# Inner products of mixer 1 on four PSUM banks, and a warm-up of TensorE in parts gated by the first tile's statistics

## Chip, cores, metric

One core of a Trainium2 chip. The metric is the device time of one launch in microseconds (us). A time quoted for a kernel is the median of its runs; a span is the length of the one profiled run, some 2 us shorter than its time. All runs used here are fast (a granted clock of 0.99 to 1.00).

## The reference, cut

```python
h  = x + linear_attention(layernorm(x), wqkv, wo)     # x: 2048 x 1024, 32 heads
h2 = h + mixer(layernorm(h), w1, b1, w2, b2)
# mixer: its own layernorm, then over the tokens:
#   u = gelu(einsum("bsd,sf->bdf", h, w1) + b1)       # "mixer 1": 2048 -> 3584
#   y = einsum("bdf,fs->bds", u, w2) + b2             # "mixer 2": 3584 -> 2048
```

## The kernel before

The matrix products run as seven block products instead of eight (Strassen-like), in two levels. A *unit* of mixer 1 makes two pairs of output tiles. Three of its outer products (1, 5 and 2) are again split in seven: these are the *inner products*, written by the class `Inner`. An inner product has the running results a, b, c and e, each 128 x 256 fp32, half a bank of PSUM (the memory that the matmuls here write to). Before the change a and e lie in one bank, b and c in another:

```python
class Inner:
    def i1(self):
        ae = psz.tile([P, BANK], F32, tag="z0", bufs=1, name="psI0")
        bc = psz.tile([P, BANK], F32, tag="z1", bufs=1, name="psI1")
        self.a, self.e, self.b, self.c = ae[:, 0:HW], ae[:, HW:CW], bc[:, 0:HW], bc[:, HW:CW]
        self.mm(1, self.a, True)                       # TensorE, 4 matmuls into a
        nc.scalar.copy(self.b, self.a)
    def i6(self): self.mm(6, self.b, False); nc.scalar.copy(self.c, self.b)
    def i2(self): self.mm(2, self.a, False); self.sink(0, 0, self.a)
    def i5(self): self.mm(5, self.e, True);  ...; nc.scalar.copy(self.es[:], self.e)
    def i7(self): self.mm(7, self.c, False); self.sink_sum(1, 1, self.c, self.es[:])  # VectorE reads c
    def i3(self): self.mm(3, self.b, False); self.sink_sum(0, 1, self.b, self.es[:])  # VectorE reads b
    def i4(self): self.mm(4, self.c, False); self.sink(1, 0, self.c)
```

`Inner2`, the third inner product of a unit, adds e to two results on VectorE instead of copying it. Matmuls of an outer product are interleaved as *fill*, so that TensorE has work while other engines read PSUM:

```python
def interleave(self, n, fs, at={}):
    steps = [(f, k) for f in fs for k in range(self.sts[0].nk)]      # 16 fill matmuls in mixer 1
    t = len(steps)
    cuts = [0, (5 * t + 8) // 16, (9 * t + 8) // 16, (12 * t + 8) // 16, t]   # groups of 5, 4, 3, 4
    ...
    for f in (n.i1, "in", 0, n.i6, n.i2, 1, n.i5, n.i7, flush, 2, "mid", n.i3, "third", 3, n.i4, "out", flush):
        ...                                                           # a number is a fill group
```

At the start, TensorE runs ten matmuls on zeros (`warm_up(10)`) while the first tile of x is loaded and normalized:

```python
def warm_up(n, w=BANK):
    tiles = [acc_tile() for _ in range(5)]
    for t in range(n):
        ps = tiles[t % 5]
        pin(nc.tensor.matmul(ps[:, 0:w], lhsT=warm[:, 0:P], rhs=warm[:, 0:w], start=True, stop=True))
...
warm_up(10)
...
ln_stats(0)          # VectorE: statistics of the two halves of tile 0, then mean and variance
```

## Time and profile before

| | before |
|---|---|
| time, median (range) | 574.38 us (574.22 to 576.22, 4 runs) |
| span of the profiled run | 572.5 us |
| TensorE busy | 561.0 us, 98% |
| one unit of mixer 1 (units 2 to 5) | 24.20 us |
| mixer 1, first inner product to mixer 2's first psE matmul | 406.93 - 241.21 = 165.72 us |

The head of the profile page of the kernel before; after each engine come its busy time, its share of the span and its instructions:

```profile
span 572.5 us, 8362 instructions
...
PE 561.0 (98%) x3136; PEld 296.6 (52%) x3136; DVE 412.2 (72%) x798; ACT 278.5 (49%) x585; POOL 1.8 (0%) x8
```

TensorE (PE) is the limit: time is to be had only from its gaps, or by taking work from it. Its waits, kernel before (what waited, for what, us in total, how often, longest):

```profile
engine line waited for: us in total, times, longest us
PE psI L209 <- DVE a L209: 4.8, 11, 0.8
PE acc_t L95 <- DVE warm L87: 1.2, 1, 1.2
PE acc_t L725 <- ACT xnT L978: 0.9, 2, 0.4
PE psI L209 <- DVE e L209: 0.5, 1, 0.5
PE tp L968 <- DVE xn L704: 0.4, 1, 0.4
PE psB L801 <- DVE xs L787: 0.3, 1, 0.3
```

The rows with psI are inner products of mixer 1 (DVE is VectorE). One of these waits in the timeline of the kernel before, in order of time (start, us, engine, line, operation, how many):

```profile
307.76 0.60 PE L209 MATMUL psI<-hi,is 128*128 128x256 f16 x4
308.05 0.67 ACT L407 ACTIVATE gO<-psC,b_sb 128x512 f16<-128x512 f32 x1
...
308.19 0.81 PE L209 MATMUL psC<-hT,wq 128*128 128x512 f16 x3
308.62 0.36 ACT L255 COPY es<-psI 128x256 f32<-128x256 f32 x1
...
309.01 0.43 DVE L209 TENSOR_TENSOR a<-psI,es 128x256 f32<-128x256 f32 x1 [1.72 <-ACT es L255]
309.35 0.68 DVE L209 TENSOR_TENSOR sa<-sa,wq 128x1024 f16<-128x1024 f16 x1
...
309.49 0.60 PE L209 MATMUL psI<-hE,is 128*128 128x256 f16 x4 [0.48 <-DVE a L209]
```

Product 7 writes c at 307.76. ScalarE (ACT) is in a gelu and copies e to `es` only at 308.62, then VectorE reads c at 309.01. Product 3, which writes only b, starts at 309.49, after this read has ended. Three fill matmuls, 216 ns apart, stood between; they started at 308.19, so product 3 could have started at 308.84.

### The profile page before, as it was taken

The numbers are of one execution on the slowest core, as the hardware profiler recorded it, in microseconds if no ns is written. First come the engines' busy times: TensorE is split into PE (matmuls) and PEld (weight loads), VectorE is DVE, ScalarE is ACT, GpSimd is POOL, SyncE is SP. The second block draws the span as 40 slices with busy tenths as digits, with TensorE's granted clock in tenths as the row PEclk, the third lists the DMA queues.
The fourth block names the chain that finished last, engine by engine and source line by source line (L and its number), as shares of the span: only waits on it lengthen the run. The fifth ranks groups of instructions, "written<-read, shape, count | busy, mean of one in ns | idle before, by whom it ended". The sixth has DMA issues, their size and how long they took to land.

```text
span 572.5 us, 8362 instructions
## 1 busy us (share of the span) xinstructions
PE 561.0 (98%) x3136; PEld 296.6 (52%) x3136; DVE 412.2 (72%) x798; ACT 278.5 (49%) x585; POOL 1.8 (0%) x8
## 2 busy tenths in 40 slices
PE   8999999999999999999999999999999999999997
PEld 3444444454444444456565565655445655655643
DVE  6898887544786798877767666684979749658725
ACT  5657777667767777535446454364220410311211
POOL 1000000000000000000000000000000000000000
PEclk9999999999999999999999999999999999999999
DMA  9933432135674931104041240413792932912111
GB/s 298 292 71 81 88 72 38 19 106 173 182 230 108 302 134 73 56 1 148 1 148 59 89 147 2 148 32 97 191 260 82 250 99 77 270 61 75 37 47 46
DMA packets 86088, 67.13 MB, mean 117 GB/s; under 512 B 15762, under 2 KB 80032, under 8 KB 86048
## 3 DMA queue, kind: packets, MB, share of 16 engines
q1 hardware_dynamic: 85312, 65.94, 40.2%
q10 hardware_dynamic: 672, 0.66, 0.3%
q8 instruction: 24, 0.39, 0.3%
q14 instruction: 16, 0.13, 0.1%
q0 software_dynamic: 64, 0.01, 0.0%
HBM read 54.54 MB, written 8.91 MB: 111 GB/s over the span
## 4 chain that ended last, share of the span: by engine, by line
PE 89%; DVE 5%; ACT 2%; DMA 1%; issue 1%; SPq 0%; DVEq 0%; ACTq 0%
PE acc_t L209 18%; PE psI L209 15%; PE psB L209 14%; PE psC L209 13%; PE psB L801 4%; PE psC L801 4%; PE psA L801 4%; PE psA L209 3%; PE psB L313 2%; PE psA L313 2%; PE acc_t L1070 2%; PE psE L801 2%; PE psC L313 2%; PE acc_t L725 2%; DVE a L209 1%; DMA x_sb<-in_A_x_dram 1%
## 5 line engine op out<-in xcount | busy, mean ns | idle before, releaser
L209 PEld LDWEIGHTS <-sa 128*128 128x128 f16 x651 | 63.7, 98 | 48.4
L209 PEld LDWEIGHTS <-wq 128*128 128x128 bf16 (+1 forms) x629 | 61.0, 98 | 46.8
L209 PEld LDWEIGHTS <-is 128*128 128x128 f16 x472 | 46.0, 98 | 29.5 <-issue 10.1
L209 PE MATMUL acc_t<-wo_sb,pqT 128*128 128x512 f16 x256 | 55.6, 379 | 0.0
L209 PE MATMUL psC<-gs,wq 128*128 128x512 f16 (+2 forms) x210 | 44.9, 365 | 0.0
L209 PE MATMUL acc_t<-xnT,wq_sb 128*128 128x512 bf16 x192 | 43.4, 379 | 0.0
L209 PEld LDWEIGHTS <-pqT 128*128 128x128 bf16 x256 | 25.0, 98 | 30.5 <-issue 0.6
L171 DVE TENSOR_SCALAR e_sb<-e_sb 128x512 bf16<-128x512 bf16 x64 | 18.6, 290 | 27.9 <-ACT e_sb L167 27.3
L167 ACT ACTIVATE e_sb<-acc_t 128x512 bf16<-128x512 f32 x40 | 23.9, 597 | 24.5 <-PE acc_t L209 12.0
L801 PEld LDWEIGHTS <-xs 128*128 128x128 f16 x208 | 20.0, 98 | 23.4 <-DVE xs L787 1.3
L209 DVE TENSOR_TENSOR ot<-ot,hr 128x512 bf16<-128x512 bf16 (+2 forms) x27 | 11.2, 414 | 28.1 <-ACT ot L454 27.7
L209 PEld LDWEIGHTS <-wq_sb 128*128 128x128 bf16 x192 | 18.5, 98 | 23.0 <-issue 1.3
L350 ACT COPY psC<-psB 128x512 f32<-128x512 f32 x22 | 12.5, 570 | 35.9 <-PE psB L209 31.1
L209 DVE TENSOR_TENSOR a<-psI,a 128x256 f32<-128x256 f32 x36 | 14.7, 423 | 20.2 <-PE psI L209 18.9
L209 PE MATMUL psB<-hT,sa 128*128 128x512 f16 x112 | 28.7, 379 | 0.0
L209 PE MATMUL psC<-hT,sa 128*128 128x512 f16 x112 | 28.3, 379 | 0.0
L209 DVE BATCH_NORM_STATS2 hst<-acc_t 128x6 f32<-128x512 f32 x32 | 21.4, 692 | 9.1 <-ACT h_bf L209 8.9
L242 ACT COPY psI<-psI 128x256 f32<-128x256 f32 x25 | 8.8, 354 | 37.9 <-PE psI L209 37.5
L801 PE MATMUL psA<-wkv,xnT 128*128 128x512 bf16 x104 | 26.7, 379 | 0.0
L209 PE MATMUL psB<-hO,sa 128*128 128x512 f16 x112 | 25.3, 379 | 0.0
L246 ACT COPY psI<-psI 128x256 f32<-128x256 f32 x25 | 8.9, 357 | 33.0 <-PE psI L209 33.0
L801 PEld LDWEIGHTS <-xnT 128*128 128x128 bf16 x156 | 15.3, 98 | 18.5 <-issue 0.2
(196 smaller groups left out, 1046.4 us busy)
## 6 DMA issues: line engine op xcount, KB each, us to landing
wq<-in_B_w_dram SPq DMA_DIRECT2D x14, 1024.0 KB, 8.0
wq<-in_B_w_dram SPq DMA_DIRECT2D x8, 1792.0 KB, 9.1
xr<-in_A_x_dram SPq DMA_DIRECT2D x16, 256.0 KB, 5.1
rdb<-rd_dram SPq DMA_DIRECT2D x32, 128.0 KB, 4.0
h_dram<-h_bf SPq DMA_DIRECT2D x16, 256.0 KB, 2.0
hr<-h_dram SPq DMA_DIRECT2D x32, 128.0 KB, 2.6
out_dram<-ot SPq DMA_DIRECT2D x31, 128.0 KB, 1.7
x_sb<-in_A_x_dram SPq DMA_DIRECT2D x15, 256.0 KB, 3.1
```

What stands on the lines that cost most here:

```text
L167: pin(nc.scalar.activation(e_sb[:], src, ACT.Exp))
L171: pin(nc.vector.tensor_scalar(e_sb[:], e_sb[:], 1.0, PHI_EPS, ALU.min, ALU.add))
L209: return (lambda *a, **kw: pin(op(*a, **kw))) if self.always or Held.on else op
L242: nc.scalar.copy(self.b, self.a)
L246: nc.scalar.copy(self.c, self.b)
L313: pe.matmul(ps[:, cols], lhsT=lhs[:, k, :], rhs=mv(k)[:, cols], start=(start and k == 0), stop=(k == self.nk - 1), skip_group_check=True,)
L350: nc.scalar.copy(self.C[:], self.B[:])
L725: mm = nc.tensor.matmul(pp[:, 0:CW], lhsT=xnT[:, kt, i * P:(i + 1) * P], rhs=wkv[:, kt, c * CW:(c + 1) * CW], start=(kt == 0), stop=(kt == ...
L801: pin(nc.tensor.matmul(ps[:], lhsT=lhs[:, k, :], rhs=rhs[:, k, :], start=(start and k == 0), stop=(k == hk2 - 1), skip_group_check=True,))
L1070: nc.tensor.matmul(qp[:, 0:SW], lhsT=wq_sb[:, kt, j * P:(j + 1) * P], rhs=xnT[:, kt, u * SW:(u + 1) * SW], start=(kt == 0), stop=(kt == ND ...
```

## The change

Its intent: with c and e in banks of their own, b and c no longer meet in one bank. The tag `w` belongs to a pool of two banks that mixer 1 used only in its first unit. Mixer 2 goes back to two banks. The first unit's sums are split so that VectorE reaches the sums of e sooner. The warm-up gets longer and is cut in parts, each behind a tiny matmul that reads x, its statistics, or its mean and variance, so that TensorE works shortly before the first tile is ready however late x comes.

```diff
     class Inner:
+        banks = 4
@@
         def i1(self):
             ae = psz.tile([P, BANK], F32, tag="z0", bufs=1, name="psI0")
             bc = psz.tile([P, BANK], F32, tag="z1", bufs=1, name="psI1")
-            self.a, self.e, self.b, self.c = ae[:, 0:HW], ae[:, HW:CW], bc[:, 0:HW], bc[:, HW:CW]
+            e, c = ae, bc
+            if self.banks == 4:
+                e, c = (psw.tile([P, BANK], F32, tag="w", name=f"psI{i}") for i in (2, 3))
+            self.a, self.e, self.b, self.c = ae[:, 0:HW], e[:, HW:CW], bc[:, 0:HW], c[:, HW:CW]
@@ run_first
-            before_inner()
+            before_inner(slice(0, 2))
             self.in5.mov = self.mov5
             self.interleave(self.in5, [st.p6 for st in sts])
+            before_inner(slice(2, 4))
@@ start  (warm_up(n, behind) puts one small matmul of `behind` ahead of its n)
-            warm_up(10)
+            warm_up(6)
@@
-            ln_stats(0)
+            warm_up(2, xs[0][:, 0:CW // 8])
+            ln[0] = ln_chunks(0, xs.pop(0))
+            pin(ln[0][1](0))
+            warm_up(2, ln[0][5][:, 0, :])
+            pin(ln[0][1](1))
+            pin(ln[0][2]())
+            warm_up(2, ln[0][6][:])
@@ after mixer 1
+    Inner.banks = 2
```

More of the change, by code (lines that the diff above doesn't have):

```diff
@@ L89, with warm_up, mm @@
     make_identity(nc, ident[:])
-    def warm_up(n, w=BANK):
-        tiles = [acc_tile() for _ in range(5)]
+    warm_tiles = [acc_tile() for _ in range(5)]
+    def warm_up(n, behind=None):
+        def mm(lhsT, rhs):
+            ps = warm_tiles[0]
+            warm_tiles.append(warm_tiles.pop(0))
+            pin(nc.tensor.matmul(ps[0:lhsT.shape[-1], 0:rhs.shape[-1]], lhsT=lhsT, rhs=rhs, start=True, stop=True))
+        if behind is not None:
+            mm(behind, behind)
         for t in range(n):
-            ps = tiles[t % 5]
-            pin(nc.tensor.matmul(ps[:, 0:w], lhsT=warm[:, 0:P], rhs=warm[:, 0:w], start=True, stop=True))
+            mm(warm[:, 0:P], warm[:, 0:BANK])
     maskbd = const.tile([P, P], F32)
@@ L193, in inner_moving, with sums @@
         t2, t3, t4 = (pool.tile([P, nk // 2, HW], FP16, name=f"{name}{t}")[:] for t in (2, 3, 4))
-        def sums():
-            for o, a, b in ((t3, b22, b12), (b12, b12, b11), (t2, b22, b12), (t4, b21, t2)):
+        def sums(part=slice(0, 4)):
+            for o, a, b in ((t3, b22, b12), (b12, b12, b11), (t2, b22, b12), (t4, b21, t2))[part]:
                 dve.tensor_tensor(o, a, b, ALU.subtract)
@@ L704, in norm @@
                     return nc.vector.tensor_scalar(xn[:, cs], x_sb[:, cs], mv[:, 0:1], rstd[:, 0:1], ALU.subtract, ALU.mult)
-                return xn, stats, aggr, scale, norm
+                return xn, stats, aggr, scale, norm, st, mv
             ln = {}
@@ L716, in ln_finish @@
             def ln_finish(i):
-                xn, _, _, scale, norm = ln.pop(i)
+                xn, _, _, scale, norm, _, _ = ln.pop(i)
                 for op in scale():
```

## The prediction

> **What bounds the kernel now.** The page gives TensorE 561.0 of 572.5 us busy (98%), and the chain of waits that ended last is 89% TensorE. Only TensorE's own gaps, 11.5 us, can be won back; its waits name them. At the start 2.5 us for the first memset, normalized and transposed tiles. In mixer 1: `psI` matmuls wait 11 times on the VectorE sum `a` (4.8 us) and once on `e` (0.5 us).
>
> **The mechanism in mixer 1.** a and e share one PSUM bank, b and c the other. After product 7 (into c) VectorE adds c; product 3 (into b) waits for that read though it writes other columns. The Trainium skill ("PSUM — Partial Sum Buffer", Terms) says TensorE and another engine must not be on the same bank and quadrant at once, so the guard is per bank; the trace agrees: product 3 at 285.28 and 309.49 us starts just after the sum ends. In the third inner product (Inner2) it waits for VectorE's three queued sums (1.31 us).
>
> By start times (512-column matmuls 216 ns apart, 256-column 109 ns) the three fill matmuls before product 3 start at 308.19, so it could start at 308.84; it starts at 309.49: 0.65 us lost. The second inner product loses 0.10 us so, Inner2 0.49 us (321.96 + 0.65 against 323.09). A unit (24.2 us) has 84 x 0.109 + 64 x 0.216 = 23.0 us of matmuls: the loss agrees.
>
> **What the change does.** c and e move to two banks of the pool that mixer 1 used only in its first unit. In the new instruction order product 3 has no wait; product 4 still waits on c's sum, but 1.3 us later. No mixer instruction is added. Splitting the first unit's sums moves two 0.69 us VectorE additions behind the `e` sums.
>
> **Not all of it stays.** After the first stall is gone, the next inner product's product 6 meets ScalarE: copy psB, gelu, copy a, copy b (0.38 + 0.67 + 0.37 + 0.35 us), after a VectorE sum that follows a 0.68 us `sa` addition and so hardly moves. I estimate product 6 could go at 312.09 and the copy lands at about 312.16: 0.1 us given back per unit, 0.5 in unit 1 where VectorE is fuller.
>
> Sum (estimate): unit 0 0.6; unit 1 1.1; units 2 to 5 4 x 1.1; unit 6 0.7 (its Inner2 stall was already filled): 6.9 us.
>
> **Warm-up.** 10 matmuls at 427 ns (1.20 to 5.65 us) become 12 plus three tiny ones gated by x's first half (3.46), its statistics (4.1) and the mean/variance (5.0). The gates open before TensorE gets there, so it ends at 6.1 to 6.5 instead of 5.65, against the transposes' 6.06: 0 to +0.4 us here. The skill ("TensorE: Matmul & The Clock Gate", Part 1) says a free-running window of about 3.4 us lifts the half clock; the trace's warm-up at 427 ns and later matmuls at 216 ns agree. It is insurance for a late x, perhaps against runs like 576.22. Median: +0.1.
>
> **Prediction:** 574.25 - 6.9 + 0.1 = 567.4 us, range 565.6 to 569.6; faster by over 2%: 0.01, within 2%: 0.97, slower: 0.02.
>
> **Right if** the waits of TensorE lose the `a`/`e` rows, a unit takes 23.1 us, PE busy stays 561. **Wrong if** ScalarE's chain holds product 6 for as long as the old stall, the pool's tiles are released late, or the clock wakes later.

## The result

| | before | after |
|---|---|---|
| time, median (range) | 574.38 us (574.22 to 576.22) | 566.93 us (566.61 to 567.74) |
| ratio of fast runs | | 0.9865, 95% interval 0.9843 to 0.9888 |
| span of the profiled run | 572.5 | 566.0 |
| TensorE busy | 561.0 | 558.1 |
| one unit of mixer 1 | 24.20 | 22.98 |
| mixer 1, as above | 165.72 | 400.40 - 242.28 = 158.12 |

A ratio here is the mean time of one kernel's fast runs over that of the other's fast runs of the same rounds, so it is not quite the ratio of the medians.

The same head and waits, kernel after (its helper lines have moved from L209 to L216):

```profile
span 566.0 us, 8365 instructions
...
PE 558.1 (99%) x3127; PEld 296.6 (52%) x3143; DVE 411.3 (73%) x798; ACT 277.4 (49%) x585; POOL 1.8 (0%) x8
```

```profile
engine line waited for: us in total, times, longest us
PE acc_t L738 <- ACT rstd L714: 1.7, 1, 1.7
PE acc_t L97 <- DVE warm L87: 1.2, 1, 1.2
PE acc_t L738 <- ACT xnT L991: 0.5, 1, 0.5
PE psB L814 <- DVE xs L800: 0.3, 1, 0.3
```

All waits of psI are gone; what this view still shows lies in the first 36 us. The stall shown before, now in the timeline of the kernel after:

```profile
305.69 0.60 PE L216 MATMUL psI<-hi,is 128*128 128x256 f16 x4
...
306.12 0.81 PE L216 MATMUL psC<-hT,wq 128*128 128x512 f16 x3
306.55 0.36 ACT L267 COPY es<-psI 128x256 f32<-128x256 f32 x1
...
306.77 0.60 PE L216 MATMUL psI<-hE,is 128*128 128x256 f16 x4
306.94 0.43 DVE L216 TENSOR_TENSOR a<-psI,es 128x256 f32<-128x256 f32 x1 [1.72 <-ACT es L267]
...
307.21 1.03 PE L216 MATMUL psC<-hT,wq 128*128 128x512 f16 x4
...
308.07 0.60 PE L216 MATMUL psI<-hi,wq 128*128 128x256 f16 x4
```

Product 3 starts at 306.77, 0.65 us after the first fill matmul, before VectorE has begun to read c. Product 4, which writes c again, starts at 308.07, when the read (306.94 to 307.37) is over.

The units by stretches. Columns: stretch, its length, then for each engine its busy time and instructions, granted clock, DMA share, GB/s. First the kernel before, then after:

```profile
300.62:324.82 24.20, 23.40 (x150) 14.48 (x148) 16.41 (x36) 11.91 (x27) 0.00 (x0) 1.00 0.27 87
324.82:349.02 24.20, 23.40 (x150) 14.45 (x148) 16.40 (x36) 11.91 (x27) 0.00 (x0) 1.00 0.28 88
```

```profile
298.54:321.52 22.98, 22.98 (x150) 14.48 (x148) 16.23 (x36) 11.74 (x28) 0.00 (x0) 1.00 0.30 93
321.52:344.51 22.99, 22.99 (x151) 14.49 (x148) 16.22 (x36) 11.75 (x28) 0.00 (x0) 1.00 0.29 92
```

The same 150 matmuls took 24.20 us and take 22.98, with TensorE busy all the time. Its busy time fell by 0.42 us a unit though its work did not change: before, each stall began with a modelled tail of the last matmul that counts as busy. That is why the waits named only 5.3 us in mixer 1, while 7.60 came back.

The profiled run after is the slowest of its four, 567.74 us against 566.61 to 566.94. Its first projection matmul starts at 8.32 us, against 7.19 before. The wait is put down to `rstd` of ScalarE at 8.00 us, which is tile 1's and on which that matmul does not depend. It needs the copies `xnT` of tile 0, which end at 7.44 us, and the first half of the weights wkv, issued at 1.18 us, which took 7.0 us to land in this run and 5.1 in the run before. So some 1.1 us of this profiled run is a late transfer, and it is not part of the mixer's gain.

### The profile page after: what moved, and what is told of

Same layout as the page of the kernel before. It is cut to its first block, busy times and chain, and to the rows that moved or that the text cites. A ratio compares the mean times of both kernels' runs of the same rounds, so it can differ in the third digit from the quotient of the medians.

```text
span 566.0 us, 8365 instructions
## 1 busy us (share of the span) xinstructions
PE 558.1 (99%) x3127; PEld 296.6 (52%) x3143; DVE 411.3 (73%) x798; ACT 277.4 (49%) x585; POOL 1.8 (0%) x8
## 4 chain that ended last, share of the span: by engine, by line
PE 96%; DVE 2%; ACT 1%; issue 1%; DMA 0%
PE acc_t L216 18%; PE psI L216 16%; PE psC L216 15%; PE psB L216 15%; PE psA L216 4%; PE psC L814 4%; PE psB L814 4%; PE psA L814 4%; PE acc_t L738 3%; PE psA L325 2%; PE psB L325 2%; PE acc_t L1089 2%; PE psE L814 2%; PE psC L325 2%; PE kvps L767 1%; PE psE L325 1%
## 5 line engine op out<-in xcount | busy, mean ns | idle before, releaser
L216 PEld LDWEIGHTS <-sa 128*128 128x128 f16 x651 | 63.7, 98 | 48.5 <-issue 0.2
L216 PEld LDWEIGHTS <-wq 128*128 128x128 bf16 (+1 forms) x629 | 61.1, 98 | 46.8
L216 PEld LDWEIGHTS <-is 128*128 128x128 f16 x472 | 46.1, 98 | 21.6 <-DVE hi L216 0.4
L216 PE MATMUL acc_t<-wo_sb,pqT 128*128 128x512 f16 x256 | 55.6, 379 | 0.0
L216 PE MATMUL psC<-gs,wq 128*128 128x512 f16 (+2 forms) x210 | 45.0, 365 | 0.0
L216 PE MATMUL acc_t<-xnT,wq_sb 128*128 128x512 bf16 x188 | 43.1, 379 | 0.2
L216 PEld LDWEIGHTS <-pqT 128*128 128x128 bf16 x256 | 25.0, 98 | 30.5 <-issue 0.6
L216 DVE TENSOR_TENSOR ot<-ot,hr 128x512 bf16<-128x512 bf16 (+2 forms) x27 | 11.2, 414 | 28.1 <-ACT ot L466 27.7
L216 PEld LDWEIGHTS <-wq_sb 128*128 128x128 bf16 x192 | 18.5, 98 | 23.0 <-issue 1.3
L216 PE MATMUL psB<-hT,sa 128*128 128x512 f16 x112 | 28.7, 379 | 0.0
L216 PE MATMUL psC<-hT,sa 128*128 128x512 f16 x112 | 28.3, 379 | 0.0
L216 DVE BATCH_NORM_STATS2 hst<-acc_t 128x6 f32<-128x512 f32 x32 | 21.4, 692 | 9.1 <-ACT h_bf L216 8.9
L216 DVE TENSOR_TENSOR a<-psI,a 128x256 f32<-128x256 f32 x36 | 14.7, 422 | 17.9 <-PE psI L216 17.2
L216 PE MATMUL psB<-hO,sa 128*128 128x512 f16 x112 | 25.3, 379 | 0.0
```

The lines of the kernel that those rows point to most:

```text
L216: return (lambda *a, **kw: pin(op(*a, **kw))) if self.always or Held.on else op
```

## Experiments

Each kernel was timed in five rounds beside the kernel before (4 to 6 runs of each) and gave a correct result. e1, e3 to e6, e8 and e10 are the changed kernel with the old warm-up put back and, but for e1, one thing more edited; e2, e9, e11 and e12 keep the gated warm-up; e7 is built on the kernel before. "Mixer 1" is the stretch of the tables above, from the profiled run.

| run | time, median (range) | ratio to before | mixer 1 |
|---|---|---|---|
| e1 banks and split only | 566.65 (566.47 to 566.86) | 0.9868 | 158.12 |
| e2 gated warm-up only | 574.75 (574.26 to 574.95) | 1.0007 | 165.73 |
| e3 only c moved | 566.76 (566.64 to 566.80) | 0.9869 | 158.13 |
| e4 only e moved | 573.85 (573.49 to 573.93) | 0.9991 | 165.20 |
| e5 banks without the split | 566.70 (566.61 to 567.61) | 0.9862 | 158.13 |
| e6 Inner2 back on two banks | 569.33 (569.04 to 570.79) | 0.9910 | 160.57 |
| e7 two banks, fill cut anew | 569.18 (568.97 to 571.71) | 0.9909 | 160.61 |
| e8 x late, old warm-up | 571.38 (570.86 to 571.75) | 0.9945 | |
| e9 x late, gated warm-up | 570.26 (570.08 to 571.37) | 0.9932 | |
| e10 x later, old warm-up | 575.23 (575.18 to 575.27) | 1.0013 | |
| e11 x later, gated warm-up | 574.08 (573.30 to 574.57) | 0.9993 | |
| e12 gated warm-up, two matmuls shorter | 566.70 (566.65 to 566.96) | 0.9869 | |

### Which part carries the gain: e1 and e2

```diff
 # e1, on the changed kernel
-            warm_up(6)
+            warm_up(10)
-            (the gated parts)
+            ln_stats(0)
```

> The banks and the split of the first unit's sums, with the warm-up of before. Theory (the banks carry it all): 566.8 to 567.1 us, ratio to before 0.9865 within 0.001; mixer 1 from the first inner product to the last product 3 takes 148.2 us as in the changed kernel (before: 156.2). Rival (the gated warm-up carries part): above 567.9 us.

Measured 566.65 us, ratio 0.9868. That is 0.15 us below the expected range, which was set around the 566.93 of the change; the ratio is as expected. The expectation's 148.2 us is another stretch than the table's: it fits the end of the last product 4 (389.10 + 0.44 - 241.34 = 148.20 us in e1, and 156.2 in the kernel before). It is 8.0 us shorter and the table's only 7.60, because before, two of mixer 2's matmuls (0.43 us) already ran ahead of the last product 3 and so filled part of that wait.

```diff
 # e2, on the changed kernel
-        banks = 4
+        banks = 2
-            before_inner(slice(0, 2))
+            before_inner()
-            before_inner(slice(2, 4))
```

> The gated warm-up alone, two banks, sums unsplit. Theory: 574.2 to 574.6 us, ratio 1.000 within 0.001, and all of the eleven waits of TensorE on the sum a (4.8 us by the profile) stay. Rival: 573.5 us or less, or the slow single runs near 576 vanish while before still shows them in the same rounds.

Measured 574.75 us, ratio 1.0007 (0.9993 to 1.0020), a little over the range that was expected; all eleven waits on `a` (4.8 us) are there. So the banks with the split carry the gain, and the warm-up carries none of it. It may cost something: the trace of e2 shows TensorE still warming up when the first tile is ready. Start of e2 on TensorE:

```profile
1.19 2.74 PE L97 MATMUL acc_t<-warm 128*128 128x512 bf16 x6 [1.19 <-DVE warm L87]
3.87 0.26 PE L97 MATMUL acc_t<-x_sb 128*64 128x64 bf16 x1
4.06 1.03 PE L97 MATMUL acc_t<-warm 128*128 128x512 bf16 x2
5.02 0.20 PE L97 MATMUL acc_t<-st 128*6 128x6 f32 x2
5.16 0.99 PE L97 MATMUL acc_t<-warm 128*128 128x512 bf16 x2
6.08 0.19 PE L97 MATMUL acc_t<-mv 128*2 128x2 f32 x2
6.20 0.60 PE L97 MATMUL acc_t<-warm 128*128 128x512 bf16 x2
6.64 0.61 PE L980 MATMUL tp<-ident,xn 128*128 128x128 bf16 x8
```

The transposes of tile 0 start at 6.64 us with no wait. In e1 they start at 6.11, and there TensorE had waited 0.46 us for the tile. The difference in time, 0.5 us between e2 and before (574.24 in these rounds) and 0.3 between the change (566.93, from other rounds) and e1, points the same way, but the intervals of the ratios do not separate them. Nor does the trace of the change show this cost: there the same warm-up matmuls ran at full speed already from 4.06 us, and the transposes started at 5.94 us.

### Which bank: e3 and e4

```diff
 # e3
-                e, c = (psw.tile([P, BANK], F32, tag="w", name=f"psI{i}") for i in (2, 3))
+                c = psw.tile([P, BANK], F32, tag="w", name="psI3")
 # e4
+                e = psw.tile([P, BANK], F32, tag="w", name="psI2")
```

> Three banks: only c moves to a bank of its own, e stays beside a; warm-up of before. Theory (product 3 waited only because b shares its bank with c, which VectorE reads): the whole gain, 566.8 to 567.3 us, no wait of TensorE on the VectorE sums in mixer 1. Rival (e beside a costs too, both have to move): 569 to 572 us with a wait of product 5 or of product 1 in its place.

> Three banks: only e moves, c stays beside b; warm-up of before. Theory: nothing is gained, 574.0 to 574.8 us, and product 3 waits for the sum of c at the same places, 0.3 to 0.8 us each. Rival (any further bank helps): 570 us or less.

e3: 566.76 us (0.04 below the range), the whole gain, and no psI row among TensorE's waits. e4: 573.85 us, and the waits are those of before, less one:

```profile
PE psI L216 <- DVE a L216: 4.8, 11, 0.8
```

So what cost was c beside b: a read of c by VectorE against a matmul that writes b in the same bank. A bank more that does not part them leaves the waits standing; e beside a costs nothing. The 0.4 us of e4 was not expected. It is the twelfth wait, that on `e` in the first unit: product 3 comes 4.98 us after the unit's first inner matmul, where it came 5.51 after it before. e4 still carries the split of the sums, and its trace shows what that does: in the kernel before, VectorE reads c at 246.25 us, behind two additions of 0.69 us that started at 244.91; in e4 these two come after the sums of e, and it reads c at 245.63. So the split has a worth while b and c share a bank; e5 asks whether it has one with four banks.

### The split of the sums: e5

```diff
-            before_inner(slice(0, 2))
+            before_inner()
             ...
-            before_inner(slice(2, 4))
```

> Four banks, warm-up of before, the first unit's four moving sums in one piece again. Theory (with c in its own bank no matmul waits for VectorE's e sums, so their place in VectorE's queue does not matter): as the banks with the split, 566.5 to 567.0 us. That the split has a worth of its own was seen with e moved alone, where unit 0's wait was gone and 0.4 us with it. Rival (the split is needed with four banks too): 567.2 us or more, a wait of 0.3 us or more in unit 0.

Measured 566.70 us and 158.13 us for mixer 1, as e1. With c in its own bank no matmul waits for those sums, and the split does nothing.

### Do the stalls add: e6

```diff
     class Inner2(Inner):
+        banks = 2
```

> Four banks for the first two inner products of a unit, two banks for Inner2, warm-up of before. Theory, from the start times of before: five stalls of 0.49 us come back (units 1 to 5; unit 6 fills its own with mixer-2 matmuls), 2.4 us: 568.9 to 569.3 us. Rival (the stalls run together, and giving one back costs nothing because another engine sets the pace of a unit): under 568 us; or (a unit's stalls add to more than their parts): over 570 us.

Measured 569.33 us, 0.03 above the range; mixer 1 takes 160.57, that is 2.45 us more than e1, against 2.4 expected. The profile's five waits sum to only 1.6 us:

```profile
PE psI L216 <- DVE a L216: 1.6, 5, 0.3
```

The loss per stall, counted from start times (0.49 us), adds up; the idle time of the waits view (0.3 us each) understates it.

### Covering the wait instead of removing it: e7

```diff
 # on the kernel before
             cuts = [0, (5 * t + 8) // 16, (9 * t + 8) // 16, (12 * t + 8) // 16, t]
+            if fs[0].__self__.nk == NSP:
+                cuts = [0, 5, 8, 13, t]
```

> The kernel before, two banks, with only the four groups of fill matmuls of mixer 1 cut anew: 5, 3, 5, 3 of the sixteen instead of 5, 4, 3, 4, so two more (0.43 us) stand between product 7 and product 3. Theory (the stall is time between product 7 and VectorE's read, to be covered by any work): 0.43 us less in each long stall, small new waits of product 5 (0.05 us), so 4 to 5 us gained: 569.3 to 570.4 us. Rival (the pace of a unit is set by ScalarE or VectorE, and the banks help by something else): within 1 us of 574.2.

Measured 569.18 us, a shade better than the range. Without any bank, only by putting two more fill matmuls between product 7 and product 3, mixer 1 falls to 160.61 us: 5.1 of the 7.6 us. This is a second and independent sign that the stall was nothing but the time from product 7 to the end of VectorE's read of c, with too little other work for TensorE in it. What stays is the rest of the stalls in unit 1 (a wait of 0.6 us) and in unit 0 (0.3) and small gaps of 0.03 to 0.07 us elsewhere: product 5, for instance, starts at 305.45 us where it could at 304.77 + 3 x 0.216 = 305.42, since one fill matmul less stands before it.

### What the gated warm-up is for: e8 to e11

In the profiled runs of before and after, x came in time (statistics from 3.46 and 3.34 us). To see the warm-up at work, x's first tile was put late:

```diff
+            pin(nc.scalar.dma_start(wkv[:, 0:hk, 0:CW], ...))      # 1 MB of weights ahead of x
+            pin(nc.sync.dma_start(wkv[:, hk:ND, 0:CW], ...))
             xs = {0: load_x(0, True)}
             xs[1] = load_x(1)
-            (the same two loads, here before the change of order)
 # e8: old warm-up, e9: gated warm-up; e10 and e11: the next 1 MB of wkv goes ahead of x as well
```

> Four banks, warm-up of before, x's first tile issued behind 1 MB of wkv, so that it lands some 2.5 us later (estimate from 0.5 MB in 5.1 us and x's 2.7 us before). The warm-up ends at 5.65 us and TensorE then has nothing until about 8.5. Theory (the gated warm-up is insurance for a late x): TensorE's clock falls back in this gap in some runs, matmuls of the first tile at 427 ns apart instead of 216, and the time spreads by 1 us or more over the runs. Rival (a gap of 3 us does not put the clock back): first matmuls at 216 ns, all runs within 0.5 us.

> The same late x with the gated warm-up. Theory: TensorE idles from 3.8 us to x's arrival, then works up to the transposes; first matmuls of the first tile 216 ns apart, time under that of the ungated kernel by 0.3 us or more, and with less spread. Rival: no difference, or slower by 0.3 us as with x in time.

> As e8, but x issued behind 2 MB of wkv, some 5 us late; TensorE idle from 5.65 us to about 11. Theory: the clock is back at half speed in every run, the first eight matmuls of tile 0 take 3.4 us instead of 1.9.

> As e9, but x issued behind 2 MB of wkv. Theory: the gated matmuls run for about 2.4 us before the transposes and may or may not raise the clock in time; if they do, the first eight matmuls take 1.9 us and the kernel beats the ungated one by 1 to 2 us; if not, they are equal within 0.5 us.

Start of TensorE in e8, then e9:

```profile
1.19 4.45 PE L97 MATMUL acc_t<-warm 128*128 128x512 bf16 x10 [1.19 <-DVE warm L87]
9.04 0.92 PE L981 MATMUL tp<-ident,xn 128*128 128x128 bf16 x8 [3.40 <-DVE xn L717]
10.11 3.22 PE L738 MATMUL acc_t<-wkv,xnT 128*128 128x512 bf16 x8 [0.15 <-ACT xnT L991]
13.16 0.61 PE L981 MATMUL tp<-ident,xn 128*128 128x128 bf16 x8
```

```profile
8.81 1.03 PE L97 MATMUL acc_t<-warm 128*128 128x512 bf16 x2
9.64 1.06 PE L981 MATMUL tp<-ident,xn 128*128 128x128 bf16 x8
10.95 2.33 PE L738 MATMUL acc_t<-wkv,xnT 128*128 128x512 bf16 x8 [0.25 <-ACT xnT L991]
13.12 0.61 PE L981 MATMUL tp<-ident,xn 128*128 128x128 bf16 x8
```

In e8 the warm-up ended at 5.65 us; the eight matmuls of tile 0 then take 3.22 us where they took 1.90 before. The granted clock of e8 in short stretches (the same columns as in the unit table) shows why:

```profile
9.20:9.40 0.20, 0.20 (x5) 0.10 (x4) 0.20 (x2) 0.00 (x0) 0.00 (x0) 1.00 1.08 343
9.40:9.60 0.20, 0.20 (x4) 0.20 (x4) 0.20 (x1) 0.13 (x1) 0.00 (x0) 0.50 1.06 338
```

The clock fell to half at 9.4 us, 3.75 us after the modelled end of the last warm-up matmul and 0.36 us after TensorE had begun again. The Trainium skill ("TensorE: Matmul & The Clock Gate", Part 1) says the array falls back to half clock after at least one idle window of about 3.4 us; e8, where TensorE was idle for 3.40 us, agrees. In e10 less was enough: by the record its clock fell at 8.15 us, 2.9 us after the modelled end of the last warm-up matmul (5.26 us). With the gated warm-up (e9) the eight matmuls take 2.33 us: by their spacing, the clock rose during them. My expectation of 216 ns for all of them was missed, and so were both spreads: e8 spans 0.9 us instead of 1 or more, and e9 spans 1.3, not less. The medians, 571.38 against 570.26 us, differ by 1.1 us in favour of gating, but the ranges overlap, and so do the intervals of the ratios (0.9933 to 0.9958 and 0.9919 to 0.9944). The traces do not show this gain: in e9 the eight matmuls start 0.84 us later, and the transposes after them start at 13.12 us against 13.16. These two profiled runs (the fastest of e8, the second slowest of e9) have spans of 569.1 and 569.0.

With x later still the case is clear: e10 575.18 to 575.27 us, e11 573.30 to 574.57. The first tile's eight matmuls and the third tile's transposes, in e10 and then in e11:

```profile
13.91 3.60 PE L738 MATMUL acc_t<-wkv,xnT 128*128 128x512 bf16 x8 [0.25 <-ACT xnT L991]
22.07 0.61 PE L981 MATMUL tp<-ident,xn 128*128 128x128 bf16 x8
```

```profile
14.21 2.34 PE L738 MATMUL acc_t<-wkv,xnT 128*128 128x512 bf16 x8 [0.25 <-ACT xnT L991]
20.91 0.61 PE L981 MATMUL tp<-ident,xn 128*128 128x128 bf16 x8
```

The eight matmuls take 3.60 us in e10 and 2.34 in e11, though the gated kernel starts them 0.3 us later; by the third tile it is 1.16 us ahead. As expected of every run, all five of e10 show the slower clock: a mean of 0.991, against 0.999 to 1.000 in e11. So the gated warm-up is insurance: it is worth about 1.1 us (575.23 - 574.08) if x is as late as here, and may cost some tenths when x is in time. How often x comes late by itself was not measured.

### A shorter gated warm-up: e12

```diff
 # on the changed kernel
-            warm_up(2, xs[0][:, 0:CW // 8])
+            warm_up(1, xs[0][:, 0:CW // 8])
-            warm_up(2, ln[0][5][:, 0, :])
+            warm_up(1, ln[0][5][:, 0, :])
```

> The changed kernel with two warm-up matmuls less, one behind x and one behind its statistics: 6 + 1 + 1 + 2 instead of 6 + 2 + 2 + 2, so ten in all as before the change, still gated. Theory (with x in time the gated warm-up costs only by running past the point where the first tile is ready, 6.64 us against 6.1 in the warm-up run): the transposes start at 6.2 us or earlier even when the clock wakes late, and the time is that of the banks alone, 566.5 to 566.8 us. Rival (the small gated matmuls or the broken rhythm cost): transposes after 6.4 us, 566.9 us or more.

Measured 566.70 us; the transposes start at 6.10 us after a wait of 0.29. That is the time of e1, the gating kept, but it is not a proof that it beats the change: 566.65 to 566.96 against 566.61 to 567.74, from different rounds. In this run the clock also rose early (the matmul at 4.68 us is at full speed), so its worst case was not seen. Its worth with a late x was not tried.

## Why the prediction was right

- **What bounds the kernel.** Right: TensorE was busy all along, and the time won is its gaps. One number of this step was off: "PE busy stays 561". It fell to 558.1 (558.7 in e1), because a gap's first 0.16 us or so had counted as busy. And "Only TensorE's own gaps, 11.5 us" was the profile's idle time, which understates the gaps; it did no harm, as the sum was made from start times.
- **The mechanism.** Right, and shown twice over: c alone in a bank of its own gives the whole gain (e3), e alone leaves eleven of the twelve waits (e4), and covering the wait by other work gives two thirds of the gain without any bank (e7). The Trainium skill ("PSUM — Partial Sum Buffer", Terms) has the rule that TensorE and another engine must not be on one bank and quadrant at once; the trace shows the wait that the program's guard for it makes. Whether the chip would have failed without the guard was not tried. Nor do the runs tell a guard by bank from one by tile: wherever b and c shared a bank, they were halves of one tile too.
- **The size of each stall.** Right: 0.65, 0.10 and 0.49 us a unit make 1.24, and a unit became 1.22 us shorter. The 0.49 of Inner2 was tested alone: five of them, 2.45 us (e6).
- **"Not all of it stays."** The mis-sized term. I took off 0.5 us in unit 1 and 0.1 us in each later unit (1.0 us in all) for ScalarE's chain of copies. In the units that the unit table shows nothing is given back: in the unit from 298.54 ScalarE's copy of b ends at 309.92, and product 6 starts at 310.02, just when its fill ends (five matmuls from 308.94). So that copy lands 0.10 us before it is needed, where I had put it 0.07 us after: my estimate was about 0.2 us too late. In unit 1, TensorE waits 0.17 us for a copy of psB. Unit by unit the gain was 0.63 us (unit 0), 1.29 (unit 1), 1.22 in each of units 2 to 5, and 0.80 (unit 6): 7.60 us instead of 6.9.
- **The warm-up.** "0 to +0.4 us" is not contradicted: the medians of e2 and e1 put its cost at 0.3 to 0.5 us without resolving it, and the trace of the change shows none. "Insurance for a late x" is right for the very late x of e10 and e11; for e8 and e9 it is not settled. That it prevents runs like 576.22 is not shown: such runs came up again in later rounds of the kernel before (576.12, 576.72), and the profile was never taken in one. What makes them slow stays open.
- **The sum.** 574.24 - 7.60 = 566.64 us for the banks (e1 measured 566.65); the change itself stands 0.3 above that, at 566.93, in other rounds; whether that is the warm-up is not resolved. The prediction of 567.4 is 0.5 too high: it took 0.7 us too little for mixer 1, mostly by giving back too much in units 1 to 5, and added 0.1 where 0.3 stands. (Its own terms for the units add to 6.8, not 6.9.)

## What to carry to other kernels

When TensorE waits in a kernel that is otherwise full, look at which halves of a PSUM bank meet: in this kernel a matmul into one half waited for VectorE's read of the other half (0.65 us at 309.49 us). Part the pair that meets in time (here c and b, not e and a), or move independent matmuls into the time of the read. Count what a stall costs from the starts of the matmuls, not from the idle time, which begins at a modelled end.

## What the Trainium skill lacked or had wrong

- "Perfetto Trace Analysis" (Tensor Engine Instruction) says that the profiler estimates a matmul's end. It does not say what follows for reading waits: five stalls of 0.49 us by start times stood as 0.3 us each in the waits (e6), and the busy time of TensorE in a unit was 23.40 us with stalls and 22.98 without, for the same matmuls.
- "TensorE: Matmul & The Clock Gate" (Seeing it yourself) warns that records of the clock gate are unreliable. Not there: from the start of the kernel to the first change the granted clock stood at 1.00 in these traces while the warm-up matmuls ran at 427 ns (e2: 4.06 us and 5.16 us, two in 1.03 and 0.99). Only the spacing of matmuls tells.
- The same page (Part 1) says that the point of the clock's rise varies by 500 ns either way. Here it varied by more: in the changed kernel the warm-up matmuls were at full speed from 4.06 us, in e2 two of them were still 427 ns apart at 4.06 and full speed came only by 6.20, with the same instructions ahead of them.
- That page does not say how much matmul work an idle window may hold before the clock stays up: by the record the clock fell 0.36 us after TensorE had begun again in e8, and 2.9 us after the end of the last warm-up matmul in e10.
- No page says that a wait for several semaphores can be put down to the wrong one, as in the view used here: the wait at 8.32 us in the profile after was for the weights, landing 7.0 us after their issue at 1.18, and was booked on ScalarE's `rstd`.
